# Feed-forward matmuls as two column tiles of 64, and full-width K weights in the scores, in a fused attention and feed-forward kernel

## The chip, the cores and the metric

The kernel runs on one core of one Trainium2 chip. The metric is the device time in microseconds of one execution; lower is better. A run that is more than 1.5% above the fastest of its kernel counts as slow and is left out of ratios (one run of the kernel before, 583.82 us, is such a one; why it was slow is not known). One execution of each kernel was recorded by the hardware profiler; its span, from first to last instruction, is about 2 us shorter than its own time.

## The reference

```python
# q, k, v: (8 batches, 12 heads, 448 tokens, 64)
scores = matmul(q, k.T) / sqrt(64)
attn   = maximum(scores, 0)**2 / 448
x      = matmul(attn, v)                 # heads side by side: (3584, 768)
xn     = x / sqrt(mean(x*x) + 1e-6) * rms_g
g, val = xn @ w_gate, xn @ w_val         # 768 -> 1536
out    = (silu(g) * val) @ w_out         # 1536 -> 768
```

## The kernel before

All products use bf16 operands. A head has 64 dimensions, so the kernel treats two heads at a time, and its matmuls come in three shapes of the 128 x 128 array:

- Scores contract over 64 rows. The two heads of a pair sit in the two row halves of the array and run side by side, started 3 ns apart ("row tiles"). A chunk of 112 of the 448 keys is the stationary operand, the *weights* of the array; the 448 queries stream past it.
- Attention times V (AV) contracts over 112 keys and gives 64 outputs per head. The two heads sit in the two column halves ("column tiles").
- The feed-forward network (FFN) uses the whole array: 128 contracted rows, 128 outputs.

For the first two batches TensorE also transposes q and k, in tiles of 64 columns; for the others a transfer does it.

The work of attention for batch b+1 is cut into small units and dealt out between the feed-forward groups of batch b, so that TensorE always has something to do. That is why the three shapes alternate all through the kernel. The excerpts below are cut and joined; the whole kernel follows.

```python
# scores: two row tiles; q is stored before k in qkT
for hh in range(2):
    prt = slice(hh * D, (hh + 1) * D)
    nc.tensor.matmul(out=psS[:, hh, :S],
        lhsT=qkT[b][prt, j, 1, c * PC : (c + 1) * PC],     # 112 columns
        rhs=qkT[b][prt, j, 0, :], start=True, stop=True)

# attention times V: two column tiles (unchanged)
for c in range(NCH):
    for hh in range(2):
        nc.tensor.matmul(out=psAV[hh * D : (hh + 1) * D, :],
            lhsT=ld["v", b][:, 2 * j + hh, c * D : (c + 1) * D],
            rhs=rsq[b, j, c][:, hh, :], start=(c == 0), stop=(c == NCH - 1))

# norm: sum of squares, the full array (unchanged)
for kt in range(KT):
    nc.tensor.matmul(out=psSS[:], lhsT=ones_bf[:], rhs=x2s[b][:, kt, :], ...)

# gate and value projections, the full array; outproj() is built the same way
for kt in range(KT):
    nc.tensor.matmul(out=ps[:], lhsT=w_sb[:, kt, fb * P : (fb + 1) * P],
        rhs=xns[b][:, kt, :], start=(kt == 0), stop=(kt == KT - 1))

# the units of attention for one pair of heads j (cut)
add(0.5, lambda j=j: scores(b, j, (0, 1)))
add(1.2, lambda j=j: scores(b, j, (2, 3)), lambda j=j: j and attend(b, j - 1))
```

## Time and profile before

| | before |
|---|---|
| time, median (4 runs, the slow one among them) | 482.23 us |
| time, the three fast runs | 481.55 to 482.41 us |
| profiled span | 480.2 us |
| TensorE busy | 96% |
| TensorE's share of the chain that ended last | 89% |

These are lines of the page of the kernel before. Part 1 gives busy microseconds and share of the span for each engine; part 4 follows the chain of work that ended last. PE is TensorE's matmuls, PEld its weight loads.

```profile
PE 462.3 (96%) x2872; PEld 220.8 (46%) x2872; DVE 284.5 (59%) x449; ACT 253.7 (53%) x380; POOL 55.7 (12%) x48
...
PE 89%; DVE 6%; ACT 2%; issue 1%; DMA 1%; POOL 0%; DVEq 0%; ACTq 0%; POOLq 0%
```

The stretches view of the same kernel gives busy time per engine in each stretch of 50 us.

```profile
150.00:200.00 50.00, 50.00 (x302) 23.68 (x300) 33.59 (x53) 30.22 (x45) 5.52 (x3) 1.00 0.81 93
200.00:250.00 50.00, 50.00 (x301) 23.86 (x300) 32.24 (x51) 29.02 (x44) 5.54 (x3) 1.00 0.84 94
```

The first number after the length is PE: TensorE is busy for every microsecond, while VectorE (the third) and ScalarE (the fourth) have about a third of their time free, or more. But "busy" doesn't mean that the array streams data at its best rate: matmuls are pipelined, and their ends are modelled. What can be trusted is the *start* of each matmul. The distance from one start to the next is called the pitch here, and the sum of the pitches is the time.

The groups view of TensorE, with shapes kept apart, names the three shapes (rows\*columns of the array). The two numbers after the bar are busy time and the mean length of one in ns, which includes the pipeline and so is longer than the pitch.

```profile
L297 PE MATMUL psG<-xn,wg_sb 128*128 128x448 bf16 x576 | 128.4, 357 | 5.7 <-DVE xn L286 5.3
L323 PE MATMUL psO<-wo_sb,hT 128*128 128x512 bf16 x336 | 77.1, 379 | 0.0
L200 PE MATMUL psS<-qkT 64*112 64x448 bf16 x384 | 57.8, 372 | 4.2 <-ACT r L214 3.5 <-DVE qkT L179 0.7
L229 PE MATMUL psAV<-r,vb 112*64 112x448 bf16 x384 | 46.2, 359 | 0.8 <-DVE r L217 0.8
...
L297 PEld LDWEIGHTS <-wg_sb 128*128 128x128 bf16 x576 | 52.2, 98 | 69.0 <-issue 25.9 <-DVE xn L286 1.7
L200 PEld LDWEIGHTS <-qkT 64*112 64x112 bf16 x384 | 18.4, 124 | 40.0 <-issue 36.2 <-DVE r L217 1.5 <-DVE qkT L179 0.9
L229 PEld LDWEIGHTS <-vb 112*64 112x64 bf16 x384 | 17.8, 109 | 25.0 <-issue 16.7 <-DVE r L217 1.1
```

The timeline view of TensorE shows the pitches at work. Columns: start in us, length in us, then the group of like matmuls that ran from there.

```profile
119.62 0.59 PE L200 MATMUL psS<-qkT 64*112 64x448 bf16 x4
120.14 0.95 PE L229 MATMUL psAV<-r,vb 112*64 112x448 bf16 x8
121.02 1.31 PE L297 MATMUL psV<-xn,wv_sb 128*128 128x448 bf16 x6
122.16 1.30 PE L297 MATMUL psG<-xn,wg_sb 128*128 128x448 bf16 x6
123.39 0.59 PE L200 MATMUL psS<-qkT 64*112 64x448 bf16 x4
123.91 1.31 PE L297 MATMUL psV<-xn,wv_sb 128*128 128x448 bf16 x6
125.05 1.30 PE L297 MATMUL psG<-xn,wg_sb 128*128 128x448 bf16 x6
```

Read the differences of the first column. A feed-forward group of six matmuls lasts 1.14 us, 189 ns each, when it is followed by another (122.16 - 121.02). The same group lasts 1.23 us when scores follow it (123.39 - 122.16). AV has four pairs of 189 ns, 0.76 us, but takes 0.88 us until the feed-forward goes on (121.02 - 120.14). Scores have two pairs, 0.38 us, but take 0.52 us. These extra tenths at the borders between shapes are what the change is after.

### The profile page before, as it was taken

What the parts mean: (1) busy time and instruction counts of PE and PEld (TensorE: products, weight loads), DVE (VectorE), ACT (ScalarE), POOL (GpSimd) and SP (SyncE); (2) the same over time, 40 slices, a digit from 0 to 9 for tenths busy, and PEclk for the clock granted to TensorE, in tenths of its full rate; (3) what the DMA queues carried; (4) which work ended last, traced back from release to release, by engine and by line L of the source; (5) the groups of instructions that cost most, each with busy time, mean ns of one, the idle gap of its engine ahead of it and who ended that gap; (6) DMA issues with size and microseconds to landing.
All of it is one profiled execution on the core that took longest, in us unless ns stands there. A gap on an engine that the chain in (4) does not pass through costs nothing.

```text
span 480.2 us, 7118 instructions
## 1 busy us (share of the span) xinstructions
PE 462.3 (96%) x2872; PEld 220.8 (46%) x2872; DVE 284.5 (59%) x449; ACT 253.7 (53%) x380; POOL 55.7 (12%) x48
## 2 busy tenths in 40 slices
PE   7977999899999999999999999999999999999995
PEld 3322444444445444454445544454445544455553
DVE  3875388567673767557663776656663676752210
ACT  4871366465565556465564566465654566552221
POOL 8463001420004000030003000000000000000000
PEclk9997999999999999999999999999999999999999
DMA  9999999999005990099203990078001300021013
GB/s 107 199 204 199 209 162 147 156 200 146 0 2 81 216 125 0 1 179 161 46 2 59 217 147 0 1 129 141 3 0 42 91 1 0 1 66 34 0 34 98
DMA packets 128032, 43.32 MB, mean 90 GB/s; under 512 B 100608, under 2 KB 124416, under 8 KB 128000
## 3 DMA queue, kind: packets, MB, share of 16 engines
q0 software_dynamic: 88944, 23.60, 51.4%
q1 hardware_dynamic: 39056, 19.28, 20.8%
q8 instruction: 22, 0.36, 0.3%
q14 instruction: 10, 0.08, 0.1%
HBM read 47.19 MB, written 11.01 MB: 121 GB/s over the span
## 4 chain that ended last, share of the span: by engine, by line
PE 89%; DVE 6%; ACT 2%; issue 1%; DMA 1%; POOL 0%; DVEq 0%; ACTq 0%; POOLq 0%
PE psG L297 24%; PE psV L297 24%; PE psO L323 22%; PE psS L200 9%; PE psAV L229 8%; PE psSS L274 2%; DVE r L217 2%; DVE xn L286 2%; DVE rstd L283 1%; ACT r L214 1%; DMA kb<-in_k_dram 1%; DVE r L212 1%; PE psT L174 1%; PE psB L139 0%; ACT rstd L279 0%
## 5 line engine op out<-in xcount | busy, mean ns | idle before, releaser
L214 ACT ACTIVATE r<-psS 112x896 bf16<-112x896 f32 x147 | 128.5, 915 | 52.1 <-PE psS L200 51.9
L297 PE MATMUL psG<-xn,wg_sb 128*128 128x448 bf16 x576 | 128.4, 357 | 5.7 <-DVE xn L286 5.3
L297 PE MATMUL psV<-xn,wv_sb 128*128 128x448 bf16 x576 | 126.1, 355 | 0.0
L314 DVE TENSOR_TENSOR hT<-sil,psV 128x448 bf16<-128x448 bf16 x96 | 59.6, 621 | 101.5 <-PE psV L297 100.1
L323 PE MATMUL psO<-wo_sb,hT 128*128 128x512 bf16 (+1 forms) x672 | 113.1, 326 | 0.0
L217 DVE TENSOR_TENSOR r<-r 112x896 bf16<-112x896 bf16 x189 | 109.9, 627 | 0.4 <-ACT r L214 0.3
L308 ACT ACTIVATE sil<-psG 128x448 bf16<-128x448 f32 x96 | 52.3, 544 | 85.5 <-PE psG L297 85.5
L323 PEld LDWEIGHTS <-hT 128*128 128x128 bf16 x672 | 64.8, 98 | 47.4 <-issue 4.1
L297 PEld LDWEIGHTS <-wg_sb 128*128 128x128 bf16 x576 | 52.2, 98 | 69.0 <-issue 25.9
L297 PEld LDWEIGHTS <-wv_sb 128*128 128x128 bf16 x576 | 54.3, 98 | 57.6 <-issue 10.4
L330 ACT COPY ost<-psO 128x512 f32<-128x512 f32 (+1 forms) x56 | 26.7, 477 | 71.4 <-PE psO L323 71.4
L200 PE MATMUL psS<-qkT 64*112 64x448 bf16 x384 | 57.8, 372 | 4.2 <-ACT r L214 3.5
L212 DVE TENSOR_SCALAR r<-psS 112x896 bf16<-112x896 f32 x45 | 48.9, 1087 | 17.5 <-PE psS L200 17.5
L229 PE MATMUL psAV<-r,vb 112*64 112x448 bf16 x384 | 46.2, 359 | 0.8 <-DVE r L217 0.8
L200 PEld LDWEIGHTS <-qkT 64*112 64x112 bf16 x384 | 18.4, 124 | 40.0 <-issue 36.2
L283 DVE RECIPROCAL rstd<-rstd 128x448 f32<-128x448 f32 x8 | 23.6, 2953 | 22.2 <-ACT rstd L279 22.2
L240 ACT ACTIVATE xT<-psAV 128x448 bf16<-128x448 f32 x48 | 26.1, 544 | 10.8 <-PE psAV L229 7.2
L93 POOL DMA_DIRECT2D vb<-in_v_dram x9 | 8.1, 901 | 204.3 <-PE psAV L229 151.9
L286 DVE SCALAR_TENSOR_TENSOR xn<-xT,g_sb,rstd 128x448 bf16<-128x448 bf16 x48 | 29.3, 681 | 0.3
L229 PEld LDWEIGHTS <-vb 112*64 112x64 bf16 x384 | 17.8, 109 | 25.0 <-issue 16.7
L95 POOL DMA_DIRECT2D qb<-in_q_dram x6 | 13.8, 2304 | 33.2 <-DMA qkT<-kb 32.1
L95 POOL DMA_DIRECT2D kb<-in_k_dram x6 | 15.1, 2511 | 7.5 <-PE psV L297 6.4
(43 smaller groups left out, 119.5 us busy)
## 6 DMA issues: line engine op xcount, KB each, us to landing
qb<-in_q_dram POOLq DMA_DIRECT2D x7, 672.0 KB, 13.8
kb<-in_k_dram POOLq DMA_DIRECT2D x7, 672.0 KB, 21.0
vb<-in_v_dram POOLq DMA_DIRECT2D x7, 672.0 KB, 9.2
out_dram<-ost SPq DMA_DIRECT2D x8, 336.0 KB, 5.3
wg_sb<-in_moe_w_gate_dram POOLq DMA_DIRECT2D x4, 576.0 KB, 18.5
wv_sb<-in_moe_w_val_dram POOLq DMA_DIRECT2D x4, 576.0 KB, 20.1
wo_sb<-in_moe_w_out_dram POOLq DMA_DIRECT2D x2, 1152.0 KB, 26.1
out_dram<-ost SPq DMA_DIRECT2D x8, 288.0 KB, 4.7
```

Source lines behind the costliest of these rows:

```text
L95: nc.gpsimd.dma_start(out=t[:].rearrange("p c (h d) -> p c h d", d=D)[:, :, h0:h1, :], in_=src.rearrange("h (p c) d -> p c h d", c=NCH),)
L200: nc.tensor.matmul(out=psS[:, hh, :S], lhsT=qkT[b][prt, j, 1, c * PC : (c + 1) * PC], rhs=qkT[b][prt, j, 0, :], start=True, stop=True,)
L212: nc.vector.tensor_relu(out=r[:], in_=psS[:, :, :S])
L214: nc.scalar.activation(out=r[:], in_=psS[:, :, :S], func=ACT.Relu)
L217: lambda r=r, eng=eng: eng.tensor_tensor(out=r[:], in0=r[:], in1=r[:], op=ALU.mult)
L229: nc.tensor.matmul(out=psAV[hh * D : (hh + 1) * D, :], lhsT=ld["v", b][:, 2 * j + hh, c * D : (c + 1) * D], rhs=rsq[b, j, c][:, hh, :], st ...
L283: nc.vector.reciprocal(out=rstd[:], in_=rstd[:])
L286: nc.vector.scalar_tensor_tensor(out=xn[:, kt, :], in0=xTs[b][:, kt, :], scalar=g_sb[:, kt : kt + 1], in1=rstd[:], op0=ALU.mult, op1=ALU.mult,
L297: nc.tensor.matmul(out=ps[:], lhsT=w_sb[:, kt, fb * P : (fb + 1) * P], rhs=xns[b][:, kt, :], start=(kt == 0), stop=(kt == KT - 1),)
L308: nc.scalar.activation(out=s[:], in_=psG[:], func=ACT.Silu)
L314: nc.vector.tensor_tensor(out=hTs[b // 2][:, fb, o : o + S], in0=sil[b, fb][:], in1=psV[:], op=ALU.mult)
L323: nc.tensor.matmul(out=ps[:, :w], lhsT=hTs[i][:, fk, t * P : (t + 1) * P], rhs=wo_sb[:, fk, o : o + w], start=(fk == 0), stop=(fk == FT - 1),)
```

## The change

The intent: the feed-forward takes AV's shape, so that the border between AV and the feed-forward is no longer a change of shape; and the K weights get 128 columns instead of 112, so that they load the way full-width weights do. The 16 extra columns produce rows that nobody reads; k is put before q so that the last chunk can read past its end into q.

```diff
--- before.py
+++ after.py
@@ -102,7 +102,7 @@
 
     def transpose_dma(b):
         new_qkT(b)
-        for ti, nm in enumerate(("q", "k")):
+        for ti, nm in enumerate(("k", "q")):
             for c in range(NCH):
                 nc.sync.dma_start_transpose(
                     out=qkT[b][:, :, ti, c * PC : (c + 1) * PC], in_=ld[nm, b][:, c, :]
@@ -168,7 +168,7 @@
         if j == 0:
             new_qkT(b)
         psT = ps_m.tile([P, 2, S], BF16, name="psT", tag="mm")
-        for ti, nm in enumerate(("q", "k")):
+        for ti, nm in enumerate(("k", "q")):
             for c in range(NCH):
                 for hh in range(2):
                     nc.tensor.transpose(
@@ -192,15 +192,16 @@
             pending.pop(0)()
 
     def scores(b, j, cs):
+
         pss = []
         for c in cs:
-            psS = ps_s.tile([PC, 2, 512], FP32, name="psS", tag="psS")
+            psS = ps_s.tile([P, 2, 512], FP32, name="psS", tag="psS")
             for hh in range(2):
                 prt = slice(hh * D, (hh + 1) * D)
                 nc.tensor.matmul(
                     out=psS[:, hh, :S],
-                    lhsT=qkT[b][prt, j, 1, c * PC : (c + 1) * PC],
-                    rhs=qkT[b][prt, j, 0, :],
+                    lhsT=qkT[b][prt, j].rearrange("p t s -> p (t s)")[:, c * PC : c * PC + P],
+                    rhs=qkT[b][prt, j, 1, :],
                     start=True,
                     stop=True,
                 )
@@ -209,9 +210,9 @@
         for c, psS in zip(cs, pss):
             r = apool.tile([PC, 2, S], BF16, name="r", tag="r")
             if relu_on(b, j, c) == "dve":
-                nc.vector.tensor_relu(out=r[:], in_=psS[:, :, :S])
+                nc.vector.tensor_relu(out=r[:], in_=psS[:PC, :, :S])
             else:
-                nc.scalar.activation(out=r[:], in_=psS[:, :, :S], func=ACT.Relu)
+                nc.scalar.activation(out=r[:], in_=psS[:PC, :, :S], func=ACT.Relu)
             eng = nc.gpsimd if square_on(b, j, c) == "pool" else nc.vector
             squares.append(
                 lambda r=r, eng=eng: eng.tensor_tensor(out=r[:], in0=r[:], in1=r[:], op=ALU.mult)
@@ -294,10 +295,11 @@
     def project(w_sb, b, fb, nm):
         ps = ps_m.tile([P, S], FP32, name=nm, tag="mm")
         for kt in range(KT):
-            nc.tensor.matmul(
-                out=ps[:], lhsT=w_sb[:, kt, fb * P : (fb + 1) * P], rhs=xns[b][:, kt, :],
-                start=(kt == 0), stop=(kt == KT - 1),
-            )
+            for h in range(0, P, D):
+                nc.tensor.matmul(
+                    out=ps[h : h + D, :], lhsT=w_sb[:, kt, fb * P + h : fb * P + h + D],
+                    rhs=xns[b][:, kt, :], start=(kt == 0), stop=(kt == KT - 1),
+                )
         return ps
 
     sil = {}
@@ -320,10 +322,11 @@
     def outproj(i, t, o, w):
         ps = ps_m.tile([P, 512], FP32, name="psO", tag="mm")
         for fk in range(FT):
-            nc.tensor.matmul(
-                out=ps[:, :w], lhsT=hTs[i][:, fk, t * P : (t + 1) * P], rhs=wo_sb[:, fk, o : o + w],
-                start=(fk == 0), stop=(fk == FT - 1),
-            )
+            for h in range(0, P, D):
+                nc.tensor.matmul(
+                    out=ps[h : h + D, :w], lhsT=hTs[i][:, fk, t * P + h : t * P + h + D],
+                    rhs=wo_sb[:, fk, o : o + w], start=(fk == 0), stop=(fk == FT - 1),
+                )
         if o == 0:
             osts[i, t] = opool.tile([P, DM], FP32, name="ost", tag="ost")
         ost = osts[i, t]
```

## The prediction

> **What bounds the kernel.** TensorE: 96% busy on the page, 89% of the chain that ended last, and busy all 50.00 us of each 50 us stretch from 150 to 400 us. The waits view gives it 12.5 us of waits, nearly all before 105 us. VectorE (59%) and ScalarE (53%) have room. So what the change does to matmul pitches after about 105 us reaches the time.
>
> **Pitches, start to start, in the ordered PE timeline.** Projections (full array, N=448) 189 ns; out-projection 216 ns (N=512) and 109 ns (N=256). Attention-times-V already runs as two 64-column tiles: a pair starts 3 ns apart and pairs follow every 189 ns, so two column tiles together cost what one full matmul costs. A change of array shape costs more: full to score (two row tiles) 282, score to full 282, score to AV 279, AV to full 285 ns: 91 to 96 ns over the pitch. (The Trainium skill, "TensorEngine Tiling (Array Packing)", Key Properties: a change of tiling mode drains the array; the trace agrees.) After a switch the second matmul is also late by the weight load that nothing hides: 11 ns for full 128-column weights, 24 for 64 columns, 45 for the 112-column K weights.
>
> **Costs and gains (estimates; transitions counted in the trace after 38.8 us):**
> - 41 AV-to-FFN changes are no longer a switch: 41 x (96+11) = -4.4 us.
> - 7 FFN-to-AV entries: 7 x (93+24) = -0.8 us.
> - Batch 1's TensorE transposes use 64 columns too; 11 boundaries with the FFN, about 110 ns each: -1.2 us, partly in a stage that waits anyway.
> - K weights of 128 columns should load by the fast path (skill, "TensorE: Matmul & The Clock Gate", Weight-path perf modes: on for 128 weights; this trace's 128-column loads show it as 4 chunks of 32): late second pair 45 to about 12 ns, 84 score units: -2.7 us. The 16 extra columns cost no streaming time.
> - Score-to-FFN, 48 times, enters with 64-column loads: +0.6 us.
> - The norm's sum-of-squares matmuls stay full array between column-tiled FFN matmuls: 14 new switches: +1.5 us.
> - FFN streaming itself: unchanged, 1824 matmuls become 1824 pairs at 189/216/109 ns.
> Sum about -7 us; I credit 6.5.
>
> **Risk.** Matmuls grow from 2872 to 4696, with as many loads: four instructions per 189 ns, four per 109 ns for N=256. The trace shows such rates only in bursts (transposes: four per 49 ns, 32 in a row); sustained, only 58 ns per instruction over 500. If the queue can't be fed at 47 ns each, the FFN slows and the result is a clear loss. I give that about 10%.
>
> **Prediction:** 476 us, 80% range 470 to 482. Faster by over 2%: 0.10; within 2%: 0.80; slower by over 2%: 0.10.
>
> **What the profile would show.** Right: FFN pairs 3 to 4 ns apart at 189/216/109; AV-to-FFN gap near 186 instead of 285; score-to-FFN still near 280; second score pair near 200 instead of 230, score loads near 98 ns in 4 chunks of 32 instead of 124; sum-of-squares entered and left at about 93 ns over pitch. Wrong: pairs slower than that in long FFN runs or N=256 runs (instruction supply or weight loads); AV-to-FFN still 280 (112 and 128 rows not one mode); score loads not in chunks.
>
> **What would make it wrong:** instruction supply; two tiles reading the same moving operand colliding; a lower granted clock (0.992 now).

## The result, and the profile after

The time went from 482.23 us (median of 4, one of them slow; 482.04 for the three fast runs) to 475.66 us (median of 4: 475.6 to 476.89). The ratio of the two is 0.9875 with a 95% interval from 0.9852 to 0.9897. (Ratios are the mean time of one kernel's fast runs over that of the other's in the same rounds, so not quite the ratio of the medians.) That is a gain of 1.25% (1.0 to 1.5%; some 6.0 us), within the 2% that separates "same" from "faster" here, but clear of noise. The profiled span fell from 480.2 to 473.7 us.

The same lines of the page of the changed kernel:

```profile
PE 455.2 (96%) x4696; PEld 246.7 (52%) x4696; DVE 283.5 (60%) x449; ACT 254.1 (54%) x380; POOL 55.7 (12%) x48
...
PE 89%; DVE 5%; ACT 2%; DMA 1%; issue 1%; POOL 0%; DVEq 0%; ACTq 0%; POOLq 0%
```

TensorE is still the bound, with 1824 more matmuls and as many more loads (4696 against 2872). Its busy share tells nothing of the gain: 96% before, 96% after.

The groups view of TensorE of the changed kernel:

```profile
L299 PE MATMUL psG<-xn,wg_sb 128*64 128x448 bf16 x1152 | 129.5, 357 | 5.1 <-DVE xn L287 5.1
L326 PE MATMUL psO<-wo_sb,hT 128*64 128x512 bf16 x672 | 77.4, 379 | 0.0
L201 PE MATMUL psS<-qkT 64*128 64x448 bf16 x384 | 54.4, 354 | 4.6 <-ACT r L215 3.7 <-DVE qkT L179 0.7
L230 PE MATMUL psAV<-r,vb 112*64 112x448 bf16 x384 | 46.1, 358 | 1.0 <-DVE r L218 1.0
...
L299 PEld LDWEIGHTS <-wg_sb 128*64 128x64 bf16 x1152 | 63.8, 110 | 58.5 <-issue 20.9 <-DVE xn L287 0.4
L201 PEld LDWEIGHTS <-qkT 64*128 64x128 bf16 x384 | 12.1, 94 | 39.7 <-issue 35.7 <-DVE r L218 1.5 <-DVE qkT L179 1.2
```

The feed-forward matmuls are twice as many and their total busy time hardly changed (128.4 to 129.5 us for the gate): the two halves of a pair run at the same time. The K loads went from 124 to 94 ns although they carry more columns, while the feed-forward loads went from 98 to 110 ns although they carry half as many.

The timeline of the changed kernel, over the same pieces of work as the one shown of before:

```profile
117.72 0.55 PE L201 MATMUL psS<-qkT 64*128 64x448 bf16 x4
118.20 0.95 PE L230 MATMUL psAV<-r,vb 112*64 112x448 bf16 x8
118.98 1.30 PE L299 MATMUL psV<-xn,wv_sb 128*64 128x448 bf16 x12
120.12 1.30 PE L299 MATMUL psG<-xn,wg_sb 128*64 128x448 bf16 x12
121.36 0.55 PE L201 MATMUL psS<-qkT 64*128 64x448 bf16 x4
121.84 1.32 PE L299 MATMUL psV<-xn,wv_sb 128*64 128x448 bf16 x12
123.00 1.30 PE L299 MATMUL psG<-xn,wg_sb 128*64 128x448 bf16 x12
```

AV now takes 0.78 us until the feed-forward goes on (118.98 - 118.20), against 0.88 before: the border is gone. A visit to the scores takes 0.48 us against 0.52. A feed-forward group of six pairs takes 1.14 us, as six matmuls did. The first group after scores takes 1.16 us (123.00 - 121.84) against 1.14 before (125.05 - 123.91): the small price of 64-column loads that nothing hides.

The table adds this up over the whole trace from 45.9 us on, from the start of every matmul; it was computed from the records of the traces, and no view prints it. For each step from one pass of the array to the next (a pair counts as one pass, from the start of its first tile) the ideal pitch is taken off: N / 2.4 + 2.5 ns for N streamed columns, which the Trainium skill ("TensorE: Matmul & The Clock Gate", Back-to-back issue gap) gives for an isolated matmul. For a stream of matmuls, each with its own weight load, the same section gives about 131 ns at N = 512; these traces don't agree with that: their long runs follow at 189, 216 and 109 ns for N = 448, 512 and 256, which is the formula. What is left is listed by the kind of step. The "second pass" rows are the step from the first to the second pass after a change of work, late by the load that nothing hides: after a border the second load starts 49 ns after the first for 112-column K weights, 28 ns for 64 columns and 15 ns for full 128 columns, and the second pass is late by 44, 24 and 11 ns.

| step | count | before, us over ideal | after | each, before and after, ns |
|---|---|---|---|---|
| AV to FFN | 41 | 4.09 | 0.00 | 100, 0 |
| FFN to AV | 7 | 0.65 | 0.00 | 93, 0 |
| FFN to and from TensorE transposes | 11 | 1.06 | 0.00 | 96, 0 |
| FFN to scores | 81 | 7.56 | 8.08 | 93, 100 |
| scores to FFN | 48 | 4.64 | 4.50 | 97, 94 |
| scores to AV | 35 | 3.31 | 3.28 | 95, 94 |
| FFN to and from sum of squares | 14 | 0.00 | 1.37 | 0, 98 |
| second pass, scores | 82 | 3.62 | 0.87 | 44, 11 |
| second pass, AV | 42 | 1.01 | 0.90 | 24, 22 |
| second pass, FFN | 101 | 0.98 | 1.51 | 10, 15 |
| inside FFN runs | 1600 | -0.01 | 0.02 | 0, 0 |
| waits for other engines | 9 and 8 | 4.08 | 4.00 | |

With the few steps left out, the sum went from 31.36 to 24.81 us, -6.5 us; the span of the same two executions fell by 6.5 us. So the gain is accounted for in full by borders and exposed loads. The same sum also shows what is left: nearly 19 us of the 24.8 are the visits to the scores (their three kinds of border, and the second passes after them). And the table has its own control: before the change the feed-forward goes to the sum of squares and back 14 times, a change of work without a change of shape, and that costs 0.00 us.

### The profile page after: what moved, and what is told of

It is laid out like the page before. It is cut to its first block, busy times and chain, and to the rows that moved or that the text cites. A ratio compares the mean times of both kernels' runs of the same rounds, so it can differ in the third digit from the quotient of the medians.

```text
span 473.7 us, 10771 instructions
## 1 busy us (share of the span) xinstructions
PE 455.2 (96%) x4696; PEld 246.7 (52%) x4696; DVE 283.5 (60%) x449; ACT 254.1 (54%) x380; POOL 55.7 (12%) x48
## 4 chain that ended last, share of the span: by engine, by line
PE 89%; DVE 5%; ACT 2%; DMA 1%; issue 1%; POOL 0%; DVEq 0%; ACTq 0%; POOLq 0%
PE psG L299 24%; PE psV L299 24%; PE psO L326 22%; PE psS L201 9%; PE psAV L230 8%; PE psSS L275 2%; DVE r L218 2%; DVE rstd L284 1%; ACT r L215 1%; DMA kb<-in_k_dram 1%; DVE xn L287 1%; DVE r L213 1%; PE psT L174 1%; PE psB L139 0%; ACT rstd L280 0%
## 5 line engine op out<-in xcount | busy, mean ns | idle before, releaser
L299 PE MATMUL psG<-xn,wg_sb 128*64 128x448 bf16 x1152 | 129.5, 357 | 5.1 <-DVE xn L287 5.1
L299 PE MATMUL psV<-xn,wv_sb 128*64 128x448 bf16 x1152 | 126.7, 355 | 0.0
L326 PE MATMUL psO<-wo_sb,hT 128*64 128x512 bf16 (+1 forms) x1344 | 113.2, 326 | 0.0
L299 PEld LDWEIGHTS <-wg_sb 128*64 128x64 bf16 x1152 | 63.8, 110 | 58.5 <-issue 20.9
L326 PEld LDWEIGHTS <-hT 128*64 128x64 bf16 x1344 | 74.6, 110 | 37.5 <-issue 2.6
L299 PEld LDWEIGHTS <-wv_sb 128*64 128x64 bf16 x1152 | 65.3, 110 | 45.6 <-issue 5.2
L201 PE MATMUL psS<-qkT 64*128 64x448 bf16 x384 | 54.4, 354 | 4.6 <-ACT r L215 3.7
L201 PEld LDWEIGHTS <-qkT 64*128 64x128 bf16 x384 | 12.1, 94 | 39.7 <-issue 35.7
L243 DVE TENSOR_TENSOR x<-xT 128x448 bf16<-128x448 bf16 x48 | 18.5, 385 | 22.2 <-ACT xT L241 22.2
```

Source lines behind the costliest of these rows:

```text
L201: nc.tensor.matmul(out=psS[:, hh, :S], lhsT=qkT[b][prt, j].rearrange("p t s -> p (t s)")[:, c * PC : c * PC + P], rhs=qkT[b][prt, j, 1, :] ...
L299: nc.tensor.matmul(out=ps[h : h + D, :], lhsT=w_sb[:, kt, fb * P + h : fb * P + h + D], rhs=xns[b][:, kt, :], start=(kt == 0), stop=(kt == ...
L326: nc.tensor.matmul(out=ps[h : h + D, :w], lhsT=hTs[i][:, fk, t * P + h : t * P + h + D], rhs=wo_sb[:, fk, o : o + w], start=(fk == 0), sto ...
```

## The experiments

Theory: while TensorE is the bound, the time is the sum of the pitches, and the change acts through how many times the array changes its shape and how much of a weight load is exposed after such a change. Rivals: (A) column tiles make the feed-forward itself stream better, and the borders are a side effect; (B) all of the gain comes from the K weights or the order of q and k; (C) the wider K weights bring nothing.

### The feed-forward part alone, and the K part alone

```diff
 # e1_ffn_only: the kernel before, with only project() and outproj() as in the change
+            for h in range(0, P, D):      # two column tiles of 64
 # e2_k_only: the changed kernel, with project() and outproj() as before
-            for h in range(0, P, D):
 # (both cut)
```

> The kernel before with only the feed-forward matmuls split into two column tiles; scores untouched (112-column K weights, q before k). Theory (the time is the sum of matmul pitches, and what counts is how often the array's shape changes): boundary counts times boundary costs give -4.2 us against before, so about 478.0 us, ratio 0.991; gap from AV to FFN about 189 ns instead of 288, second score pair still about 233 ns after the first. Rival A (column tiles make the FFN itself stream faster): FFN pairs under 189 ns, and a gain of 6 us or more. Rival B (all comes from the K weights or from the swapped order of q and k): 482 us, ratio 1.00.

> The other half alone: K weights of 128 columns (and k before q), feed-forward matmuls full array as before. Theory: 84 score units save about 33 ns each where the array bounds, -2.7 us, so about 479.5 us, ratio 0.9943; second score pair 200 ns after the first instead of 233; AV to FFN still 288 ns. Rival B (all comes from here): 475.7 us, ratio 0.9875. Rival C (wider weights gain nothing): 482 us. If both halves are right, the gains of this run and of the run with the feed-forward part alone add to 6.5 to 7 us, the whole change's.

Measured in the same rounds (before: 481.69 us, median of 11): the feed-forward part alone 477.87 us, ratio 0.9923 (0.9906 to 0.9939); the K part alone 479.49 us, ratio 0.9955 (0.9931 to 0.9978). Both correct. The gains of the medians are 3.8 and 2.2 us, together 6.0; with intervals of about 1 us each way that agrees with the 6.0 us that the ratio of the whole change stands for. In these timelines each half does its own thing and leaves the other's border as it was. The feed-forward part alone:

```profile
117.50 0.95 PE L229 MATMUL psAV<-r,vb 112*64 112x448 bf16 x8
118.28 1.30 PE L298 MATMUL psV<-xn,wv_sb 128*64 128x448 bf16 x12
...
120.65 0.59 PE L200 MATMUL psS<-qkT 64*112 64x448 bf16 x4
121.17 1.32 PE L298 MATMUL psV<-xn,wv_sb 128*64 128x448 bf16 x12
```

AV to feed-forward is 0.78 us, as in the changed kernel; a visit to the scores still takes 0.52 us. The K part alone:

```profile
119.39 0.55 PE L201 MATMUL psS<-qkT 64*128 64x448 bf16 x4
119.87 0.95 PE L230 MATMUL psAV<-r,vb 112*64 112x448 bf16 x8
120.75 1.31 PE L298 MATMUL psV<-xn,wv_sb 128*128 128x448 bf16 x6
```

Here the visit takes 0.48 us, and AV to feed-forward still 0.88. Rivals B and C fall, since both halves gain. The order of q and k was not run apart from the wider K weights, which need it; but the second pass of the scores alone (3.62 to 0.86 us in this trace) makes up the K part's gain. Rival A would have needed feed-forward pairs faster than 189 ns; the long runs follow at 189, 216 and 109 ns in all four kernels.

### The gate back to the full array

If it were the column tiles that helped, then going half way should land half way. If it is changes of shape that cost, then going half way is worse than either end.

```diff
 # e3_gate_full: on the changed kernel, in project()
+        n = P if nm == "psG" else D
         for kt in range(KT):
-            for h in range(0, P, D):
+            for h in range(0, P, n):      # gate: one full matmul; value: two column tiles
```

> The changed kernel, but the gate projections stay full-array matmuls while value and output projections are two column tiles: same arithmetic, fewer instructions than the changed kernel, but a change of array shape at every turn between gate and value. Theory (a change of shape is what costs): counted boundaries give +14.2 us against the changed kernel, so about 490 us, ratio to before 1.015; gate to value and value to gate gaps about 283 ns instead of 189. Rival A (column tiles stream faster, shape changes don't matter): between before and after, 476 to 482 us.

Measured: 490.11 us (489.44 to 490.6), ratio to before 1.0173 (1.0153 to 1.0193): slower than both kernels, although it has fewer instructions than the changed one, the same arithmetic, and shapes that are each used in one of the two. The estimate from counted borders was 490. Its timeline:

```profile
121.06 0.95 PE L230 MATMUL psAV<-r,vb 112*64 112x448 bf16 x8
121.84 1.30 PE L300 MATMUL psV<-xn,wv_sb 128*64 128x448 bf16 x12
123.07 1.31 PE L300 MATMUL psG<-xn,wg_sb 128*128 128x448 bf16 x6
```

AV to value is 0.78 us (same shape), and the value group takes 1.23 us until the gate starts instead of 1.14. In the sum over all starts the steps between the full and the two-tile feed-forward, with the second passes after them, add 12.3 us. Rival A falls here: the cost is in the change of shape.

### The norm's sums as column tiles

The table above shows what the change made worse: the sum-of-squares matmuls kept the full array and became two borders each.

```diff
 # e4_norm_cols: on the changed kernel, in norm()
-            nc.tensor.matmul(out=psSS[:], lhsT=ones_bf[:], rhs=x2s[b][:, kt, :], ...)
+            for h in range(0, P, D):
+                nc.tensor.matmul(out=psSS[h : h + D, :], lhsT=ones_bf[:, h : h + D],
+                                 rhs=x2s[b][:, kt, :], ...)
```

> The changed kernel with the norm's sum-of-squares matmuls as two column tiles as well. Theory: the 14 shape changes that the change added around them go away, -1.5 us, so about 474.2 us, ratio to before 0.984; FFN to sum of squares 109 ns instead of 209 after an N=256 group, sum of squares to FFN 189 instead of 283. Rival: no change against 475.7 us, if those matmuls wait for VectorE anyway.

Measured: 473.83 us (472.9 to 475.56), ratio to before 0.9838 (0.9817 to 0.9859), correct. The changed kernel's own ratio is 0.9875, from other rounds, and the intervals overlap a little, so the times alone don't quite separate the two kernels (these five runs all lie below the changed kernel's four, 475.6 to 476.89 us). The traces show what went away. The timeline of the changed kernel around one group of sums (start, length, group):

```profile
148.31 1.31 PE L275 MATMUL psSS<-x,ones_bf 128*128 128x448 bf16 x6
149.55 5.82 PE L326 MATMUL psO<-wo_sb,hT 128*64 128x512 bf16 x64
```

And the timeline of this kernel around the same group:

```profile
147.83 1.30 PE L276 MATMUL psSS<-x,ones_bf 128*64 128x448 bf16 x12
148.97 6.22 PE L327 MATMUL psO<-wo_sb,hT 128*64 128x512 bf16 x68
```

From the start of the sums to the next matmul: 1.24 us against 1.14, which is six pitches of 189. In the sum over all starts the 14 borders around them went from 1.37 us to 0.00, and the total from 24.8 to 23.4 us. (The second passes there lost another 0.24 us, but waits for other engines grew by 0.35.)

### Four tiles of 32: was the change close to the limit of instruction supply?

The main risk that the prediction named was that TensorE might not be fed with twice the instructions. The change didn't run into it; this run asks how much room there is, and gives the border theory another test, since 32-column tiles are not AV's shape.

```diff
 # e5_four_tiles: on the changed kernel, in project() and outproj()
-            for h in range(0, P, D):
+            for h in range(0, P, 32):     # and + 32 for + D in the slices
```

> The changed kernel with every feed-forward matmul as four column tiles of 32 instead of two of 64: instructions of the feed-forward double once more (eight per 189 ns, eight per 109 ns for N=256), and its tiles no longer have AV's shape. It asks how far the change was from the limit of instruction supply, the main risk named in the prediction. Theory 1 (supply is ample; tiles of another width are another shape): the four start 3 to 4 ns apart, groups still follow at 189/216/109 ns, but AV to FFN costs about 280 ns again: +7 us against the changed kernel, about 482.5 us, ratio 1.00. Theory 2 (supply just sufficed for two tiles): groups come slower than 189 ns in long runs, N=256 slower than 109; at 30 ns per instruction the FFN alone would grow by 27%, the time to over 550 us. Theory 3 (ample, and 32 and 64 columns switch freely): 475 us.

Measured: 482.92 us (480.87 to 485.49), ratio to before 1.0022 (0.9985 to 1.006). Theory 1 put it at 482.5. The four matmuls of a group mostly start 2 to 5 ns apart, and the gap from AV to the feed-forward is back at 286 ns instead of 189. In the timeline AV takes 0.88 us until the feed-forward goes on, as before the change:

```profile
139.17 0.95 PE L230 MATMUL psAV<-r,vb 112*64 112x448 bf16 x8
140.05 6.67 PE L326 MATMUL psO<-wo_sb,hT 128*32 128x512 bf16 x144
```

The sum over all starts is 31.95 us against 24.81 of the changed kernel, +7.1 us. The end of the kernel is one long run of output projections, with nothing between. In the timeline of the kernel before it is this line (start, length, group; 512- and 256-wide matmuls are counted together):

```profile
459.46 15.76 PE L323 MATMUL psO<-wo_sb,hT 128*128 128x512 bf16 x96
```

In the timeline of the changed kernel:

```profile
453.01 15.77 PE L326 MATMUL psO<-wo_sb,hT 128*64 128x512 bf16 x192
```

And in the timeline of the kernel with four tiles:

```profile
458.36 15.77 PE L326 MATMUL psO<-wo_sb,hT 128*32 128x512 bf16 x384
```

The same work takes the same 15.8 us as 96, 192 or 384 matmuls (with as many loads). In the last case that is 768 instructions in 15.77 us, 20.5 ns each, sustained. The changed kernel needs 41 ns each in this run, so for this mix of widths it has at least a factor of two in hand. Supply is not what makes four tiles slower; the borders are.

### The filler of the first batch as column tiles

```diff
 # e6_busy_cols: on e4_norm_cols, in keep_busy()
-            nc.tensor.matmul(out=ps[:], lhsT=ones_bf[:], rhs=busy_bf[:], ...)
+            for h in range(0, P, D):
+                nc.tensor.matmul(out=ps[h : h + D, :], lhsT=ones_bf[:, h : h + D], rhs=busy_bf[:], ...)
```

> The changed kernel with the norm's sums as column tiles (as in the run of that name) and the filler matmuls of the first batch as column tiles too, so that no full-array matmul is left. Theory: at most 1.2 us of shape changes go away in the first 33 us, but TensorE waits for loads, ScalarE and VectorE there, so little of it arrives: 473 to 474 us, ratio to before 0.982 to 0.984. Rival (the start is bound by TensorE as well): 472.6 us.

Measured: 473.35 us (471.87 to 474.28), ratio 0.9816 (0.9791 to 0.9842). Its interval overlaps that of the norm's sums alone (0.9838, 0.9817 to 0.9859; other rounds, another chip). In the traces the first norm begins at 32.6 us here and at 32.7 us there, and from 45.9 us on both sums are 23.4 us: by the traces, little of the borders that went away in the first batch arrives, as expected. The run is inconclusive as to a few tenths of a microsecond, and nothing shows that the edit is needed.

One idea was not tried. All four score chunks of a head pair in a single visit would take away two borders per pair, but need twice the room for scores in PSUM, the memory that matmuls write to. No run shows what it would bring.

## Why the prediction was right

It said 476 us, 470 to 482, and a gain that stays under 2%; measured were 475.66 us and 1.25%. Point by point:

- *What bounds the kernel.* Right. TensorE's share of the chain is 89% before and after, and the whole gain is found in its pitches.
- *AV to FFN, -4.4 us.* Right: the step went from 4.09 us over ideal to 0.00, and with the second passes after it the sum is -4.4. That 112 rows used and 128 rows used are the same shape to the array was an assumption; the 0 shows it. (A first pass from one to the other costs about 4 ns in the next step, 193 instead of 189.)
- *FFN to AV, -0.8 us, and transposes, -1.2 us.* Right: -0.76 and -1.19 us with their second passes.
- *K weights, -2.7 us.* Right: second pass of the scores from 44 to 11 ns over the pitch, -2.75 us. The run with this part alone gained 2.2 us.
- *64-column loads after scores, +0.6 us.* Right: the second pass of the FFN after scores went from 10 to 24 ns over the pitch, +0.65 us over 48 visits. (The second-pass row of the FFN went up by 0.53 us only, because the vanished borders lower it.)
- *Sum of squares, +1.5 us.* Right: 1.37 us for the borders plus 0.24 for the second passes after them, and taking them away brought 1.4 us in the trace.
- *FFN streaming unchanged.* Right: 0.02 us over 1600 steps.
- *What it missed.* FFN to scores went from 93 to 100 ns over the pitch, +0.5 us over 81 visits. About half comes with each part (97 ns with the feed-forward part alone, 96 with the K part alone). The feed-forward's half is the size of the 3 to 4 ns by which the second tile of a pair starts after the first, from which the step is counted; with four tiles, whose last starts 11 ns after the first, the step is 106 ns. That fits, but no run tested it. Why the wider K weights add 3 ns is open. It is luck that this 0.5 us is the size of what the prediction held back from its sum of 7 without giving a reason.
- *Risk of instruction supply, 10%.* It didn't come true, and the four-tile run shows that it was never near.

The prediction worked because each term was a count from the trace times a distance between starts in the trace. AV had already run for a whole kernel in the shape that the feed-forward was to take, so its pitch and its borders could be read off before the change was built.

## What to carry to other kernels

When several shapes of matmul alternate on TensorE, count the borders between them and multiply by the extra distance between starts at a border, some 95 ns here: the busy share hides this completely. Bring neighbours to the same shape even at the price of twice the instructions, and take along everything that sits between them, because one group that keeps its own shape buys two borders. Where a border can't be avoided, let the side that enters have full 128-column weights where it can, since the load after it is not hidden: the second pass was late by 11 ns with them here, by 24 with 64 columns and by 44 with 112.

## What the Trainium skill lacked or had wrong

- "TensorEngine Tiling (Array Packing)", Key Properties, says that changing the tiling mode drains TensorE but gives no cost. Here it is 93 to 106 ns over the pitch, much the same between full array, two row tiles, two column tiles and four column tiles (FFN to AV 93, scores to AV 94, FFN to scores 93 to 100, AV to four tiles 97, four tiles to scores 106). It depends on the tile shape and not on rows used: 112 to 128 rows used cost 0.
- The same page, Feature Incompatibilities, says that column tiling excludes the fast weight load, and the trace is consistent with it: 64-column loads take 110 ns and are not cut in chunks, against 98 ns for 128 columns in 4 chunks. But 112-column K weights, which are no column tiles, are not cut in chunks either, so the trace can't tell the tiling from the width as the reason. The page doesn't say that row tiling keeps the fast load: 64 x 128 K weights load as 4 chunks of 32 columns and take 94 ns, against 124 ns for 64 x 112.
- "TensorE: Matmul & The Clock Gate", LDWEIGHTS, gives columns / 1.2 ns for a weight load. That would be 40 ns more for 112 columns than for 64; the records differ by 15 ns (124 against 109), and where nothing hides them, successive loads of 64 and 112 columns start 28 and 49 ns apart, about half of what it gives.
- "Perfetto Trace Analysis", Identifying the Most-Contended Engine, offers the busy share of weight loads, beside the share of peak FLOPs, as a measure of distance to the roofline. Here it rose from 46% to 52%, since the feed-forward's loads became twice as many and slower (98 to 110 ns), while the matmul pitch stayed the same and the gain came from the borders.
